# Narrower warm-up products, a moved instruction fetch and a new rule table in an attention and MLP kernel

## The chip, the core and the metric

The kernel runs on one core of a Trainium2 chip. Its engines are TensorE (PE in the profile, with its weight loads as PEld), VectorE (DVE), ScalarE (ACT), GpSimd (POOL) and SyncE (SP), which issues the DMA transfers; 16 DMA engines carry these. The time is device microseconds of one execution; the figure for a kernel is the median of several runs. The trace is of one profiled execution, whose span is a little longer than the runs without a profile.

## The reference, cut to what matters

```python
x = A_x                                        # [1, 2048, 640], bf16
xn = layernorm(x)
# attention: 32 heads of 20 columns
q, k, v = split(xn @ wqkv)                     # wqkv [640, 1920]
p = softmax(q @ k.T * 20 ** -0.5)              # 32 times 2048 x 2048
s = (p @ v).reshape(1, 2048, 640) @ wo
# token mixer: the MLP runs over the 2048 rows
h = layernorm(xn)
u = gelu(h.T @ w1 + b1)                        # w1 [2048, 1536]
y = (u @ w2 + b2).T                            # w2 [1536, 2048]
return x + s * silu(y)
```

The bulk is the exponential of 32 x 2048 x 2048 scores. ScalarE takes about three quarters of them, VectorE the rest, with an approximation that writes the bits of a bf16 number.

## The kernel before: the parts that matter here

The program is straight-line code. A scheduler written in Python decides at build time the order of each engine's instructions. It keeps a model of when each engine is free, and takes for each engine the ready candidate of the best priority.

```python
class Prog:
    def pe(self, fn, reads=(), writes=(), name="pe", cost=250.0, tail=None, w=None):
        t = self._add("pe", "pe", fn, reads, writes, name, cost=cost, tail=tail)
        self.pe_end = self.T["pe"]
        self.alog.append((t.t0, cost * 1.0 if w is None else w))
        return t

    def activity(self, T):          # modelled busy share of TensorE before T
        a = 0.0
        for t0, w in reversed(self.alog):
            if t0 < T - 3413.0:
                break
            a += w
        return a / 3413.0
```

Every 16 score tiles (WIN) one row of a table, PLAN, is read; each digit chooses the value of one option of the scheduler (slack, when a bank may be lent, and so on). The table was found by a search outside the kernel, on the model's time.

```python
    OPTS = (
        ("SLACK", (120.0, 40.0, 200.0, 320.0)),
        ("MINJ", (640.0, 320.0, 1000.0)),
        # ... (cut: 12 more)
    )
    PLAN = ("00200200000010", "02000000000000", ...)      # cut: 129 rows

    def tune(self, w):
        if w < len(self.PLAN):
            for (name, vals), i in zip(self.OPTS, self.PLAN[w]):
                setattr(self, name, vals[int(i)])
```

The model's cost of changing the way the PE array is divided, and of a DMA transpose (`nbytes` is None):

```python
        def pe_cost(mode, c):
            if pe_mode[0] != mode:
                pe_mode[0] = mode
                return c + max(0.0, (119.0 if mode == "st" else 100.0) - max(0.0, pr.T["pe"] - pr.pe_end))
            return c

        def dma(fn, reads, writes, name, nbytes, over=()):
            if nbytes is None:
                pr.dma(fn, reads=reads, writes=writes, name=name, cost=1320.0, over=over, tail=2700.0)
```

The start: x is loaded, normalized on VectorE block by block (16 blocks of 128 rows), and transposed into xnT: blocks 0 to 3 on TensorE, blocks 4 to 15 by one DMA transpose each, in batches of four. From xnT come the projections q, k and v of the first four heads; their scores are the first work for ScalarE's exponential.

```python
        def xTd_steps(b):
            dst = xnT_sb[:, :, b * 128:(b + 1) * 128]
            src = regC[:, b, :]
            return [("dma", lambda e: e.dma_start_transpose(dst, src), [S_(f"h{b}")], [S_(f"xTb{b}")], f"xTd{b}", None), ...]
```

Until then TensorE multiplies zeros to keep its clock up (`emit_warm`). Later on, where the model sees a gap and low activity, it adds products of zeros to the accumulator (`emit_fill`, four products at a time).

```python
        def emit_warm():
            pr.pe(lambda e: e.matmul(ps(AB), on_sb[:, 0:4, :], on_sb[:, :, :], start=True, stop=True),
                  reads=[S_("on")], writes=[bank_slot[AB]], name="warm", cost=pe_cost("full", 216.0) +
                  (214.0 if pr.T["pe"] < 4500.0 else 0.0), w=216.0)

        # in pe_cands, while the start lasts (ramp):
                    nxt = min([max(x[1], T) for x in c] + [1e18])
                    if not pv_seen and nxt - T > 260.0:
                        c.append((99.0, max(T, 1000.0), emit_warm))
                    elif pv_seen and nxt - T > (216.0 if pe_mode[0] == "pv" else 321.0) + self.FGAP and fill_ok() and (
                            pr.activity(T) < self.FACT):
                        c.append((99.0, T, emit_fill))
```

A last piece estimates how much work each engine has before it. The kernel stores it in `self.loads`, and nothing in the kernel calls it; the search does.

```python
        def loads():
            a, d = pr.T["act"], pr.T["dve"] + 601.0 * len(dop1)
            pe = pr.T["pe"] + 54.0 * len(avail)
            # ... (cut)
            return a - done_cost["act"], pe - done_cost["pe"], d - done_cost["dve"]
```

Of the kernel before, what the change touches and what calls it, by code (L numbers as in the profile page):

```python
# [39 lines left out]
class Prog:  # L40
# [7 lines left out]
    def __init__(self, nc, n_lanes=8):  # L48
        self.nc = nc
        self.n_lanes = n_lanes  # L50
        self.cengs = list(self.COMPUTE) + [f"d{i}" for i in range(n_lanes)]
        self.cidx_of = {c: i for i, c in enumerate(self.cengs)}
        self.tasks = {e: [] for e in self.COMPUTE}
        self.ctasks = {c: [] for c in self.cengs}
        self.gcount = 0
        self.lane_rr = 0
        self.known = {e: [0] * len(self.cengs) for e in self.COMPUTE}
        self.T = {e: 0.0 for e in self.COMPUTE}
        self.busy = {e: 0.0 for e in self.COMPUTE}
        self.pipe = 0.0  # L60
        self.pe_end = 0.0
        self.alog = []

    def lat(self, eng, src):
# [87 lines left out]
    def pe(self, fn, reads=(), writes=(), name="pe", cost=250.0, tail=None, w=None):  # L152
        t = self._add("pe", "pe", fn, reads, writes, name, cost=cost, tail=tail)
        self.pe_end = self.T["pe"]
        self.alog.append((t.t0, cost * 1.0 if w is None else w))
        return t

# [98 lines left out]
class _Kern:  # L256
# [9 lines left out]
    AB = 6  # L266
# [43 lines left out]
        ("GROT", (1, 0)),  # L310
    )
    PLAN = (
        "00200200000010", "02000000000000", "00000000000000", "00000000000010", "00000000000000", "00002200000000",
        "02002200000000", "01002200000000", "01024200101000", "00000000000000", "10000010000000", "12000010000000",
        "12203110110010", "00020010000010", "30000000000110", "30020020000110", "00020010000010", "10001400000000",
        "10001000000000", "12001010010000", "00000000000000", "02000000001000", "00000100010100", "00124100110110",
        "00124200111100", "00104300111000", "00020000000000", "00020010000000", "01020310000000", "01120310010000",
        "01010000100000", "00002200001000", "01002200001000", "10002000000000", "00000000000000", "00000300000000",
        "01004010000000", "12000210100000", "12104210100000", "00000200000000", "00121200000100", "00124200000100",
        "00124200000100", "00000400000000", "01100000000100", "00000000000000", "00000010101000", "01000010001000",  # L320
        "01000010010000", "01000010010000", "01000410010000", "02000000000110", "00020120000000", "00020220101000",
        "00220220101000", "10220210001000", "00002000000000", "00000000000000", "00102020001100", "00011200000100",
        "00000000000000", "02020200000000", "00000000000000", "10102000000010", "10100000000010", "10003000001000",
        "10003000000110", "10002300000110", "00020320000000", "20020000000000", "20220020000000", "20200020000010",
        "20200020000010", "20000320100010", "00010110100100", "01003410000000", "01003410110000", "00010000000000",
        "00002000000100", "02002000000100", "00020100000000", "00022300100000", "00000000000000", "00100000100000",
        "20100400100100", "00122010000000", "00004301010000", "00000400000010", "22001000000010", "00000000000000",
        "00000001000000", "00000200001100", "00010200000100", "10220210000000", "02100210000000", "00000020000000",
        "20013110000000", "20020310000000", "00000020110100", "00000000000000", "00003000001010", "00002100000000",
        "00002000010000", "10002020110010", "10203120100010", "02000400000000", "00110010010000", "02020000000000",  # L330
        "00110000101010", "10020000000100", "10110000010000", "00100000000000", "02120000000000", "00020020100000",
        "00020020100000", "00020100100010", "00000000000000", "00004100000010", "00000000000000", "21000400000000",
        "31020400000000", "00110201100000", "00000000100000", "02000000100010", "12000000110010", "02000020001000",
        "00000000000000", "01001000000000", "00000000000000",
    )
    PARTS = (2,)
    DX = (1, 2, 3)
# [74 lines left out]
    def schedule(self):  # L412
# [48 lines left out]
        def pe_cost(mode, c):  # L461
            if pe_mode[0] != mode:
                pe_mode[0] = mode
                return c + max(0.0, (119.0 if mode == "st" else 100.0) - max(0.0, pr.T["pe"] - pr.pe_end))
            return c

        def dma(fn, reads, writes, name, nbytes, over=()):
            if nbytes is None:
                pr.dma(fn, reads=reads, writes=writes, name=name, cost=1320.0, over=over, tail=2700.0)
            else:  # L470
                pr.dma(fn, reads=reads, writes=writes, name=name, cost=nbytes / 355.0, over=over)

# [580 lines left out]
        avail = []  # L1053
# [250 lines left out]
                      reads=[S_("zw"), S_("wp0"), S_("wp1")], writes=[bank_slot[AB]], name="pvz", cost=tot / 4, w=53.0)  # L1304
            stats["fill"] = stats.get("fill", 0) + 1

        def emit_warm():
            pr.pe(lambda e: e.matmul(ps(AB), on_sb[:, 0:4, :], on_sb[:, :, :], start=True, stop=True),
                  reads=[S_("on")], writes=[bank_slot[AB]], name="warm", cost=pe_cost("full", 216.0) +
                  (214.0 if pr.T["pe"] < 4500.0 else 0.0), w=216.0)  # L1310

        def emit_pv(items, quads):
            q = pv_pass[0]
# [595 lines left out]
            return c  # L1909

        def loads():
            a, d = pr.T["act"], pr.T["dve"] + 601.0 * len(dop1)
            pe = pr.T["pe"] + 54.0 * len(avail)
            for us, banks, grp in pexp:
                a += len(us) * 512 * 0.8335 + 50.0
                pe += 54.0 * len(us)
# [98 lines left out]
```

## Time and profile before

| | |
|---|---|
| median of 3 runs | 760.98 us (760.37 to 761.41) |
| span of the profiled execution | 762.1 us |
| granted TensorE clock, mean | 0.991 |
| products of warming (512 columns) | 27 |
| filler products | 48 |
| exponentials on ScalarE | 430 of 1024 columns, 232 of 1536 |
| score tiles on VectorE | 492 of 512 columns |

A line with busy times names the engine, its busy microseconds, and behind the x the number of instructions. The granted clock is TensorE's, as a share of full speed. In the DMA lines a queue has a number and a kind, then its packets, megabytes, and the time its packets took as a share of 16 engines; "hardware_dynamic" are the kernel's own transfers, "instruction" are packets of program code that the engines fetch while they run. A wait names the engine and line that waited, what it waited for, and us in total, times, and the longest. Line numbers are those of the kernel before; L1236 is ScalarE's exponential, L1207 the score products, L1308 the warm-up, L1302 the filler, L625 the projections q and k of the first four heads.

### The profile page before, as it was taken

The page shows a single profiled execution, that of the slowest core. Times are in us where ns is not written, and L with a number is a line of the kernel's source. Part 1 is how long each engine was busy: PE and PEld are TensorE (multiplying, and loading weights), DVE is VectorE, ACT ScalarE, POOL GpSimd, SP SyncE. Part 2 cuts the span into 40 slices and gives each one's busy share as a digit, 9 for nine tenths or more (in the row PEclk, how much of TensorE's full clock was granted, in tenths as well). Part 3 has the DMA queues.
Part 4 walks back from the last instruction along what each step waited for, and adds up shares of the span by engine and source line. Part 5 has one row for each costly group of instructions (what it writes and reads, how often), then busy time and mean ns, then how long its engine had stood idle before and what let it go on. Part 6 is the DMA issues. An engine that isn't in the chain of part 4 may idle for free.

```text
span 762.1 us, 22703 instructions
## 1 busy us (share of the span) xinstructions
PE 730.9 (96%) x10088; PEld 242.8 (32%) x10088; DVE 715.7 (94%) x1314; ACT 732.8 (96%) x684; POOL 15.9 (2%) x22
## 2 busy tenths in 40 slices
PE   8989999999999999999999999999999999999997
PEld 3332233323232323333223232333333333233322
DVE  8689999999999999999989999999999999999994
ACT  5889999999999999999999999999999999999994
POOL 4200000000000000000000000000000000000001
PEclk9899999999999999999999999999999999999999
DMA  9485110101120301211211112112133520041101
GB/s 240 62 127 132 37 35 13 43 6 36 38 62 13 74 14 38 64 31 19 69 37 20 30 44 64 43 45 66 40 80 70 116 82 13 9 144 46 47 14 69
DMA packets 117142, 42.52 MB, mean 56 GB/s; under 512 B 75300, under 2 KB 115876, under 8 KB 116996
## 3 DMA queue, kind: packets, MB, share of 16 engines
q1 hardware_dynamic: 117044, 41.07, 23.6%
q8 instruction: 79, 1.29, 0.8%
q14 instruction: 19, 0.16, 0.1%
HBM read 26.37 MB, written 10.22 MB: 48 GB/s over the span
## 4 chain that ended last, share of the span: by engine, by line
ACT 70%; PE 22%; DVE 6%; DMA 1%; issue 0%
ACT pt_sb L1236 69%; PE ps_all L1207 7%; PE ps_all L640 6%; PE ps_all L1287 6%; DVE dt_sb L1247 2%; PE ps_all L625 1%; DVE dt_sb L1271 1%; PE ps_all L925 1%; DMA xnT_sb<-regC 1%; ACT zt_sb L831 1%; ACT zt_sb L836 1%; DVE regC L940 1%; PE ps_all L733 0%; DVE regC L1606 0%; DVE bst_sb L527 0%; DMA regA<-in_A_x_dram 0%
## 5 line engine op out<-in xcount | busy, mean ns | idle before, releaser
L1236 ACT ACTIVATE pt_sb<-ps_all 128x1024 bf16<-128x1024 f32 (+1 forms) x662 | 713.8, 1219 | 8.8 <-PE ps_all L1207 7.3
L1247 DVE TENSOR_SCALAR dt_sb<-ps_all 128x512 uint16<-128x512 f32 x492 | 329.3, 683 | 19.8 <-PE ps_all L1207 18.4
L1207 PE MATMUL ps_all<-qk_sb 32*128 32x512 bf16 x2048 | 292.5, 386 | 18.0 <-ACT pt_sb L1236 13.8
L1271 DVE TENSOR_SCALAR dt_sb<-dt_sb 128x2048 uint16<-128x2048 uint16 x369 | 244.2, 685 | 1.4
L1207 PEld LDWEIGHTS ps_all<-qk_sb 32*128 32x128 bf16 x2048 | 75.8, 91 | 275.1 <-ACT pt_sb L1236 183.3
L1287 PE MATMUL ps_all<-pt_sb,v_sb 128*21 128x512 bf16 x1556 | 122.5, 383 | 0.7 <-DVE v_sb L1040 0.7
L1287 PE MATMUL ps_all<-dt_sb,vs_sb 128*21 128x512 bf16 x1476 | 123.0, 382 | 0.0
L640 PE MATMUL ps_all<-regC,regA 128*32 128x512 bf16 (+1 forms) x1536 | 69.4, 301 | 0.0
L640 PE MATMUL ps_all<-regB,regA 128*32 128x128 bf16 (+1 forms) x1536 | 68.2, 301 | 0.5 <-DVE dt_sb L1247 0.5
L640 PE MATMUL ps_all<-xnT_sb,wqk_sb 128*32 128x512 bf16 x640 | 50.1, 382 | 0.4 <-DVE zt_sb L810 0.3
L1287 PE MATMUL ps_all<-dt_sb,v_sb 128*21 128x512 bf16 x492 | 48.5, 384 | 0.7 <-DVE tr_sb L1399 0.6
L1287 PEld LDWEIGHTS ps_all<-pt_sb,v_sb 128*21 128x21 bf16 x1556 | 28.8, 90 | 49.3 <-issue 38.1
L1287 PEld LDWEIGHTS ps_all<-dt_sb,vs_sb 128*21 128x21 bf16 x1476 | 31.3, 91 | 40.3 <-issue 25.1
L640 PEld LDWEIGHTS ps_all<-regB,regA 128*32 128x32 bf16 x1536 | 28.5, 96 | 27.4 <-issue 12.3
L640 PEld LDWEIGHTS ps_all<-regC,regA 128*32 128x32 bf16 x1536 | 28.4, 96 | 26.5 <-issue 13.0
L925 PE MATMUL ps_all<-wv_sb,xnT_sb 128*128 128x128 bf16 (+3 forms) x160 | 29.7, 302 | 0.1
L1399 DVE STREAM_TRANSPOSE tr_sb<-ps_all 128x512 f32<-128x512 f32 x31 | 22.0, 710 | 0.2 <-PE ps_all L1287 0.2
L640 PE MATMUL ps_all<-wv_sb,xnT_sb 128*32 128x480 bf16 x320 | 22.0, 369 | 0.0
L640 PEld LDWEIGHTS ps_all<-xnT_sb,wqk_sb 128*32 128x32 bf16 x640 | 13.8, 95 | 19.9 <-issue 9.2
L1287 PEld LDWEIGHTS ps_all<-dt_sb,v_sb 128*21 128x21 bf16 x492 | 12.3, 90 | 24.0 <-issue 17.3
L1040 DVE CAST v_sb<-ps_all 128x480 bf16<-128x480 f32 (+1 forms) x24 | 14.3, 595 | 4.1 <-PE ps_all L733 4.1
L810 DVE TENSOR_SCALAR zt_sb<-ps_all,b2h_sb 128x512 bf16<-128x512 f32 (+1 forms) x32 | 17.0, 543 | 0.9 <-PE ps_all L640 0.8
(81 smaller groups left out, 287.8 us busy)
## 6 DMA issues: line engine op xcount, KB each, us to landing
regA<-in_B_w_dram SPq DMA_DIRECT2D x6, 1024.0 KB
regA<-in_B_w_dram SPq DMA_DIRECT2D x8, 768.0 KB
qk_sb<-qk_scratch_dram SPq DMA_DIRECT2D x56, 80.0 KB
qk_scratch_dram<-qs_sb SPq DMA_DIRECT2D x32, 128.0 KB
regA<-in_A_x_dram SPq DMA_DIRECT2D x6, 640.0 KB
ok_scratch_dram<-on_sb SPq DMA_DIRECT2D x96, 20.0 KB
out_dram<-regC SPq DMA_DIRECT2D x3, 640.0 KB
wqk_sb<-in_A_wqkv_dram SPq DMA_DIRECT2D x2, 480.0 KB
```

What stands on the lines that cost most here:

```text
L625: steps.append(("pe", lambda e, dc=dc, lhsT=lhsT: e.matmul(ps(bk, n), lhsT, xnT_sb[:, dc, tb * 512 + c0:tb * 512 + c0 + n], start=(dc == 0 ...
L640: fns.append(lambda e, c=c, e_=e_: e.matmul(oc(c, e_), lhsT[:, c:e_], rhs, start=start, stop=stop, tile_position=(0, c)))
L810: steps.append(("dve", lambda e, z=z, i=i, jj=jj: e.tensor_scalar(z[:, c0:c0 + n], ps(bk, n, i * n), 0.5, bias[:, jj:jj + 1], ALU.mult, AL ...
L831: steps.append(("act", lambda e: e.activation(tt_, tt_, AF.Tanh, scale=1.5957691216), [stt], [stt], f"th{j}", ac(n)))
L925: steps.append(("pe", lambda e, c=c, k=k: e.matmul(ap, oT_sb[0:k, c, b * 128:(b + 1) * 128], wo_ap[0:k, c, c0:c0 + n], start=(opens and c ...
L1040: return lambda e: e.tensor_copy(dst, src)
L1207: pr.pe(lambda e, outp=outp, lhsT=lhsT, rhs=rhs, g=g: e.matmul(outp, lhsT, rhs, start=True, stop=True, tile_position=(32 * g, 0)), reads=[ ...
L1236: tk = pr.act(lambda e: e.activation(outp, inp, AF.Exp, scale=math.log(2.0) / 128.0), reads=[bank_slot[b] for b in banks[:n]], writes=[S_( ...
L1247: tk = pr.dve(lambda e: e.tensor_scalar(w, src, WOFF, 0.0, ALU.add, ALU.max), reads=[bank_slot[bk]], writes=[S_(f"dt{d['tl'][0]}_{g}")], n ...
L1271: tk = pr.dve(lambda e: e.tensor_scalar(dst, src, dk, None, ALU.add), reads=[S_(f"dt{b0}_{g}") for g in range(4)], writes=[S_(f"dt{b}_{g}" ...
L1287: pr.pe(lambda e: e.matmul(outp, lhsT, rhs, start=(k == 0), stop=last, tile_position=(0, 32 * g)), reads=reads, writes=[bank_slot[AB]], na ...
L1399: steps.append(("dve", lambda e: e.transpose(tr_sb[:, :], ps(AB)), [bank_slot[AB]], [S_("tr")], f"epT{q}", 632.0))
```

## The change

The warm-up product becomes 192 columns wide instead of 512 and takes turns in three places of the bank; the scheduler's model then puts 69 of them where there were 27. As TensorE's program gets longer ahead of the first scores, the points at which it fetches its next block of instructions lie elsewhere in time. The constants of the model for changing the array's division and for the DMA transposes are set to other, measured, values. A count of moments of low activity after 45 us of modelled time goes into the search's estimate, and the table was searched anew (129 rows in both; only its first lines are shown).

```diff
+        self.low = 0
+        self.lowt = 0.0
...
     def pe(self, fn, reads=(), writes=(), name="pe", cost=250.0, tail=None, w=None):
         t = self._add("pe", "pe", fn, reads, writes, name, cost=cost, tail=tail)
         self.pe_end = self.T["pe"]
+        if t.t0 > 45000.0 and t.t0 - self.lowt > 3413.0 and self.activity(t.t0) < 0.36:
+            self.low += 1
+            self.lowt = t.t0
...
     PLAN = (
-        "00200200000010", "02000000000000", "00000000000000", "00000000000010", "00000000000000", "00002200000000",
-        "02002200000000", "01002200000000", "01024200101000", "00000000000000", "10000010000000", "12000010000000",
+        "00000000000010", "00000000000000", "00000000000010", "00000000000000", "00000410000000", "10010410000100",
+        "00004010011000", "20204010111000", "00000000000000", "02000020010010", "00000000000000", "00000010001000",
...   (all other rows, too)
-                return c + max(0.0, (119.0 if mode == "st" else 100.0) - max(0.0, pr.T["pe"] - pr.pe_end))
+                return c + max(0.0, (105.0 if mode == "st" else 113.0) - max(0.0, pr.T["pe"] - pr.pe_end))
...
-                pr.dma(fn, reads=reads, writes=writes, name=name, cost=1320.0, over=over, tail=2700.0)
+                pr.dma(fn, reads=reads, writes=writes, name=name, cost=1320.0, over=over, tail=3200.0)
...
+        nwarm = [0]
+
         def emit_warm():
-            pr.pe(lambda e: e.matmul(ps(AB), on_sb[:, 0:4, :], on_sb[:, :, :], start=True, stop=True),
-                  reads=[S_("on")], writes=[bank_slot[AB]], name="warm", cost=pe_cost("full", 216.0) +
-                  (214.0 if pr.T["pe"] < 4500.0 else 0.0), w=216.0)
+            off = 160 * (nwarm[0] % 3)
+            nwarm[0] += 1
+            pr.pe(lambda e: e.matmul(ps(AB, 192, off), on_sb[:, 0:4, :], on_sb[:, 0:6, :], start=True, stop=True),
+                  reads=[S_("on")], writes=[bank_slot[AB]], name="warm", cost=pe_cost("full", 81.0) +
+                  (80.0 if pr.T["pe"] < 4500.0 else 0.0), w=81.0)
...
         def loads():
-            a, d = pr.T["act"], pr.T["dve"] + 601.0 * len(dop1)
-            pe = pr.T["pe"] + 54.0 * len(avail)
+            lo = 1500.0 * pr.low
+            a, d = pr.T["act"] + lo, pr.T["dve"] + 601.0 * len(dop1) + lo
+            pe = pr.T["pe"] + 54.0 * len(avail) + lo
```

How the order of instructions changes: TensorE starts with 54 warm-up products (20 before), then ten transposes, 5 (2), ten transposes, 8 (3), 15 projections and one more before the first scores, as before. ScalarE has 434 exponentials of 1024 columns and 228 of 1536 and two more evictions; VectorE has 496 tiles of scores, 372 passes over four tiles (369 before) and two evictions fewer. Filler products are 100.

## The prediction

> **What bounds the kernel now.** I read the busy table first, then busy time by stage, then ScalarE's waits, then the DMA traffic of single microseconds.
>
> The page's first part, with busy time and share of the span:
>
> ```profile
> PE 730.9 (96%) x10088; PEld 242.8 (32%) x10088; DVE 715.7 (94%) x1314; ACT 732.8 (96%) x684; POOL 15.9 (2%) x22
> ```
>
> Three engines are within 2.4% of each other, so no engine can be relieved by much. What is left is idle time. The view by stage tells where (columns: stage, length, then busy time and instructions of PE, weight loads, DVE, ACT and POOL, granted clock, DMA share, GB/s):
>
> ```profile
> 0.00:13.54 13.54, 11.80 (x65) 5.19 (x66) 10.79 (x37) 4.30 (x6) 6.99 (x14) 1.00 0.88 277
> 13.54:20.55 7.01, 4.43 (x42) 2.17 (x42) 5.17 (x16) 5.54 (x5) 0.70 (x1) 1.00 1.00 146
> 20.55:28.88 8.33, 8.33 (x54) 3.13 (x53) 5.13 (x20) 6.29 (x6) 1.01 (x1) 0.59 0.24 48
> 28.88:40.21 11.33, 10.53 (x96) 4.82 (x94) 7.91 (x33) 10.62 (x10) 4.05 (x3) 1.00 0.50 73
> 40.21:47.50 7.29, 6.12 (x34) 2.15 (x35) 5.14 (x16) 4.22 (x5) 0.00 (x0) 0.77 0.73 167
> 47.50:742.00 694.50, 675.01 (x9689) 220.40 (x9686) 671.43 (x1178) 692.76 (x647) 0.88 (x1) 1.00 0.22 49
> 742.00:751.60 9.60, 9.60 (x96) 3.23 (x92) 3.10 (x5) 9.06 (x8) 0.00 (x0) 1.00 0.20 70
> 751.60:762.10 10.50, 5.05 (x26) 1.70 (x24) 6.99 (x16) 0.00 (x0) 2.26 (x2) 0.83 0.18 62
> ```
>
> Length minus ACT busy, stage by stage: 9.24, 1.47, 2.04, 0.71, 3.07, 1.74, 0.54, 10.50 us, 29.3 in all. In 694.5 us of steady state ScalarE stands still for 1.74: it sets the pace there, and the time is its work plus its idle at the two ends. Start (9.24) and tail (10.50) have the same structure in both kernels. The part that can move is the ramp from 13.54 to 47.50: 1.47 + 2.04 + 0.71 + 3.07 = 7.29 us.
>
> ScalarE's waits name score products as the ender of most of the ramp's idle:
>
> ```profile
> ACT pt_sb L1236 <- PE ps_all L1207: 7.3, 9, 1.7
> ACT qk_sb L1042 <- PE ps_all L625: 1.5, 1, 1.5
> ```
>
> Those scores need xnT, which comes in twelve DMA transposes, in batches of four (13.26 to 40.9 us). DMA by queue in five short windows: an undisturbed transpose in 27.1 to 28.2; one in 15.8 to 18.3; the middle of that, 16.7 to 18.1; one in 36.4 to 38.5; its middle, 37.2 to 38.3.
>
> ```profile
> q1 hardware_dynamic: 672, 0.16, 74.5%
> ...
> q1 hardware_dynamic: 672, 0.16, 109.1%
> q8 instruction: 1, 0.02, 3.6%
> ...
> DMA packets 29, 0.01 MB, mean 5 GB/s; under 512 B 29, under 2 KB 29, under 8 KB 29
> ...
> q1 hardware_dynamic: 672, 0.16, 111.9%
> q8 instruction: 1, 0.02, 3.1%
> ...
> DMA packets 31, 0.01 MB, mean 7 GB/s; under 512 B 31, under 2 KB 31, under 8 KB 31
> ```
>
> A transpose is 672 packets. Undisturbed ones start at 25.8, 27.1, 28.5 and 29.8: 1.35 us apart. The one met by an instruction packet at 15.8 lasts until 18.3, 2.5 us; the one met at 36.4 until 38.5, 2.1 us. In the middle of both nearly nothing moves, as if fifteen of the 16 DMA engines waited for the one that carries the instructions. So the first fetch costs batch 1 some 2.5 - 1.35 = 1.15 us, the second batch 3 some 2.1 - 1.35 = 0.75 us. Batch 1 and batch 3 are what the longest DMA pieces of the chain of waits are (4.99 us from 14.65, 2.64 us from 38.65).
>
> After both gaps in the products the granted clock falls: 0.59 in 20.55 to 28.88, 0.77 in 40.21 to 47.50.
>
> **What the Trainium skill says.** "Runtime: NRT & Kernel Launch", section "Instruction fetch mechanics": instructions come in blocks of 16 KiB, 256 instructions, on a DMA queue that the sequencer drives, and crossing a block is "mostly hidden". The trace agrees on the size (q8: 79 packets, 1.29 MB, 16.3 KB each; 2 x 10,088 product and weight-load records / 256 = 78.8); hidden it is not where a DMA transpose runs. "DMA: Bandwidth & Descriptors", section "Queues, rings and completion order": each DMA engine goes round its queues packet by packet, so a 16 KB packet stands ahead of the small ones on that engine; the trace's gap fits. "TensorE: Matmul & The Clock Gate", Part 1: half clock after a quiet window of about 3.4 us, full after a busy one. The trace agrees roughly: PE was busy 1.32 of the 3 us from 18 to 21, and from 21.5 to 27 the clock was near 0.50.
>
> **The change part by part.**
>
> *Warm-ups.* 27 products of 512 columns become 69 of 192: 42 more products, 84 more instructions with their weight loads, all but two groups of them before the first scores. The columns go from 13,824 to 13,248, so the warming work is equal: the first group ran 20 products in 5.99 us (0.43 us each cold, 0.21 warm); 54 of 192 columns are, scaled by columns, 21 x 0.16 + 33 x 0.08 = 6.0 us. It ends as before, near 7.2 to 7.4 us. Direct gain or cost: 0.
>
> *The fetch.* Before, it came when 89 products had started (15.85 us) and again after 89 + 131 = 220 (36.4 us). With the new order the 89th product is in the first projection after the warm-ups (10.62 us before). There the x and weight loads run, not a transpose; they end at 14.0 to 14.8 us, and one DMA engine's share may end up to an estimated 0.6 us later (half of the packet's 1.0 to 1.4 us, since it shares the engine), which delays batch 1 in part. I count 1.15 - 0.3 = 0.85 us won. The 220th product of the new order is in the projection of blocks 8 and 9, the one that started at 30.75 us before, as batch 2 ended (30.7). So the second fetch moves from batch 3 to the end of batch 2 or just after: of 0.75 us I count 0.6. Sum on the chain: 1.45 us.
>
> *Half clock.* With the wait in batch 1 shorter and eight filler products where four were, just at that wait, the first throttle probably goes, the second perhaps. ScalarE's idle then is 2.04 in the first slow stage; the last wait of the second, to 46.02, is 1.39. I count 1.5 us of 3.4: some of it is only moved to the wait for batch 3.
>
> *The table.* One more quad of score tiles goes to VectorE: exponentials of 1024 columns go from 430 to 434, of 1536 from 232 to 228. Busy per instruction with overlap: 431.8/430 = 1.004 and 347.0/232 = 1.496 us. ScalarE: 4 x 1.004 - 4 x 1.496 = -1.97 us, and two evictions move to it in the ramp, +0.59 + 0.38: net -1.0. VectorE: 4 x 0.669 + 3 x 0.662 = +4.7, less the evictions, to some 719 us, under ScalarE's. Filler products go from 48 to 100; 52/4 x 0.22 = 2.9 us of PE, in its gaps.
>
> *The rest.* The low-activity count and its use in the load estimate act on the search alone: nothing emitted reads them. The switching costs (105, 113) and the longer transpose tail (3200) change the order by what the scheduler believes.
>
> Sum: 1.45 + 1.5 + 1.0 = 3.95 us from 760.98: 757.0. The steady state has only 1.74 us of ScalarE idle to win and can lose more than that by a new table; I add 0.8.
>
> **The rivals.**
> 1. *The fetch only changes its victim.* It delays loads, and the second fetch hits batch 2 whole. For: the 220th product stands at the edge of batch 2; the loads run at 105% in 6 to 14 us. Against: loads do not freeze as transposes do, and batch 2 ends 4 us before batch 3 begins. The ramp gain shrinks to some 1 us, the time to 759 to 760.
> 2. *The new table is worse on the chip.* VectorE has 4.7 us more and was the chain's engine in 675 to 699; each VectorE eviction late holds a bank. For: VectorE is 94% busy; 44 of the 100 fillers stand late (products 9,625 to 9,763), so PE has gaps there. Against: ScalarE idled 1.74 us in 694.5 under the same kind of table. The time would be 761 to 763.
> 3. *The whole ramp wait goes.* Both throttles vanish and batch 3 comes early: the ramp's idle falls from 7.3 to 2, the time to 754.5.
>
> **Range and chances.** 757.8 us, 754.5 to 761.5 eight times in ten: the low end is rival 3, the high end rival 2 at its mildest, and the spread of before (760.37 to 761.41) is within it. 2% is 15.2 us, more than all the ramp's idle and the steady idle together, and slower by so much would need a new stall of 15 us: faster 0.01, within 0.98, slower 0.01.
>
> **What would show it.** The first instruction packet at 10 to 11 us with no gap in the transposes from 14.5; batch 1 done by 19.5 instead of 20.6; clock near 1.00 in 21 to 29; ScalarE's idle from its first exponential to 47.5 us between 3.5 and 5; ACT busy near 731.8. Wrong if a fetch again falls into a transpose of batch 1 or 3, if the half-clock stage stays, or if ScalarE's idle in steady state rises above 3 us.

## The result and the profile after

The changed kernel takes 757.34 us (median of 4 runs, 756.49 to 758.22) against 761.19 us for the kernel before in the same comparison (760.37 to 763.69): ratio 0.9944, 95% interval 0.9918 to 0.997. The profiled executions have spans of 756.4 and 762.1 us. The gain of 3.9 us is real and lies well within 2%.

The page's first part of the changed kernel, busy time and share of the span by engine:

```profile
PE 726.6 (96%) x10194; PEld 245.9 (33%) x10194; DVE 718.4 (95%) x1319; ACT 731.3 (97%) x686; POOL 15.7 (2%) x22
```

ScalarE has 1.5 us less work and VectorE 2.7 more, as a table that gives VectorE four more of the 2048 score tiles should make it. The view by stage of the changed kernel (columns as in the prediction: stage, length, busy time of PE, weight loads, DVE, ACT, POOL, granted clock, DMA share, GB/s):

```profile
0.00:13.54 13.54, 11.89 (x103) 9.46 (x103) 10.52 (x35) 3.75 (x5) 7.00 (x14) 1.00 0.86 277
13.54:20.55 7.01, 5.78 (x59) 2.72 (x61) 5.76 (x18) 6.94 (x7) 0.70 (x1) 1.00 0.97 146
20.55:28.88 8.33, 7.83 (x76) 3.58 (x68) 7.38 (x32) 7.94 (x9) 1.32 (x2) 1.00 0.61 77
28.88:40.21 11.33, 9.64 (x88) 4.38 (x86) 7.99 (x32) 9.75 (x11) 3.74 (x3) 1.00 0.67 145
40.21:47.50 7.29, 7.22 (x64) 2.69 (x62) 7.21 (x16) 7.29 (x8) 0.00 (x0) 1.00 0.64 77
47.50:742.00 694.50, 673.96 (x9742) 219.63 (x9741) 672.38 (x1177) 691.85 (x648) 0.63 (x1) 1.00 0.22 49
```

Length minus ACT busy: 9.79 in the start, 0.07 + 0.39 + 1.58 + 0.00 = 2.04 in the ramp, 2.65 in the steady state. Before it was 9.24, 7.29 and 1.74. So, between these two executions, the ramp gave 5.25 us, the start took 0.55 and the steady state 0.9 back; with 1.5 us less work and 0.4 less idle at the end that makes the 5.7 us between the two spans. The clock column has no 0.59 and no 0.77 any more. ScalarE's wait for scores, 7.3 us in nine times before, in the changed kernel:

```profile
ACT pt_sb L1241 <- PE ps_all L1212: 2.9, 4, 1.3
```

The fetch did not do what I had counted on. DMA by queue in three short windows of the changed kernel: 14.6 to 15.1 us, 16.5 to 17.5 us, and 28.2 to 30.8 us:

```profile
q8 instruction: 1, 0.02, 13.4%
...
DMA packets 69, 0.03 MB, mean 26 GB/s; under 512 B 61, under 2 KB 69, under 8 KB 69
...
q8 instruction: 1, 0.02, 3.7%
```

The first instruction packet starts at 14.95 us, at the very edge of batch 1. In the second window 61 packets of a transpose and 8 larger ones, of the loads of x, move in a whole microsecond: the last load packet ends at 17.1 us (before: 14.95), and the first transpose, under way since 15.1, ends at 17.6. Batch 1 is done at 20.6 us, exactly as before. The second fetch, at 28.36 us, falls into the last transpose of batch 2 and makes it last from 28.2 to 30.8.

What closed the wait instead is seen in the timeline of PE. The kernel before (start, length, engine, line, operation, count, and in brackets the idle time before it and what ended it):

```profile
16.88 0.39 PE L1207 MATMUL ps_all<-qk_sb 32*128 32x512 bf16 x2 [0.17 <-ACT pt_sb L1236]
19.68 0.50 PE L625 MATMUL ps_all<-xnT_sb,wp_sb 128*128 128x256 bf16 x3 [2.41 <-DMA xnT_sb<-regC]
20.11 0.39 PE L1207 MATMUL ps_all<-qk_sb 32*128 32x512 bf16 x3
```

And the changed kernel:

```profile
17.44 0.39 PE L1212 MATMUL ps_all<-qk_sb 32*128 32x512 bf16 x2 [0.20 <-ACT pt_sb L1241]
17.75 0.61 PE L1307 MATMUL ps_all<-wp_sb,zw_sb 128*21 128x512 bf16 x8
18.78 0.39 PE L1212 MATMUL ps_all<-qk_sb 32*128 32x512 bf16 x3 [0.41 <-ACT pt_sb L1241]
19.72 0.72 PE L630 MATMUL ps_all<-xnT_sb,wp_sb 128*128 128x256 bf16 x5 [0.55 <-DMA xnT_sb<-regC]
```

The data for the projection (L625, now L630) come at the same moment, 19.7 us. But before, the projection stood ahead of three scores that needed no transpose, and held them and ScalarE up. Now those scores and eight fillers stand ahead of it. VectorE's order differs likewise: before, the cast of the second part of this projection stood ahead of four normalizations, now two of them stand ahead of it (VectorE before):

```profile
23.90 0.42 DVE L1040 CAST qk_sb<-ps_all 128x256 bf16<-128x256 f32 x1 [1.89 <-PE ps_all L625]
24.24 1.51 DVE L545 TENSOR_SCALAR regC<-regA,st_sb 128x640 bf16<-128x640 bf16 x4
```

The place of the scores comes from the scheduler's constants (a transpose is believed to land 500 ns later; tail_only below has the same three scores ahead), which I had counted as nothing. The eight fillers come with the narrow warm-ups: warm_only has them, all_but_warm doesn't.

### The profile page after: what moved, and what is told of

Read it like the earlier page. It is cut to its first block, busy times and chain, and to the rows that moved or that the text cites. A ratio compares the mean times of both kernels' runs of the same rounds, so it can differ in the third digit from the quotient of the medians.

```text
span 756.4 us, 22917 instructions
## 1 busy us (share of the span) xinstructions
PE 726.6 (96%) x10194; PEld 245.9 (33%) x10194; DVE 718.4 (95%) x1319; ACT 731.3 (97%) x686; POOL 15.7 (2%) x22
## 4 chain that ended last, share of the span: by engine, by line
ACT 67%; PE 23%; SPq 4%; DVE 3%; DMA 3%; POOL 1%; issue 0%; DVEq 0%; ACTq 0%
ACT pt_sb L1241 65%; PE ps_all L1212 7%; PE ps_all L1292 7%; PE ps_all L645 7%; SPq L906 3%; DMA xnT_sb<-regC 1%; PE ps_all L930 1%; DMA regA<-in_B_w_dram 1%; ACT zt_sb L836 1%; DMA wqk_sb<-in_A_wqkv_dram 1%; DVE dt_sb L1252 1%; PE ps_all L630 1%; POOL st_sb L567 0%; SPq L1425 0%; DVE regC L1615 0%
## 5 line engine op out<-in xcount | busy, mean ns | idle before, releaser
L1252 DVE TENSOR_SCALAR dt_sb<-ps_all 128x512 uint16<-128x512 f32 x496 | 330.8, 681 | 17.1 <-PE ps_all L1212 15.6
L1212 PE MATMUL ps_all<-qk_sb 32*128 32x512 bf16 x2048 | 286.6, 384 | 18.7 <-ACT pt_sb L1241 14.5
L1212 PEld LDWEIGHTS ps_all<-qk_sb 32*128 32x128 bf16 x2048 | 73.9, 91 | 276.4 <-ACT pt_sb L1241 193.0
L645 PE MATMUL ps_all<-regC,regA 128*32 128x512 bf16 (+1 forms) x1536 | 65.9, 301 | 0.0
L645 PE MATMUL ps_all<-wv_sb,xnT_sb 128*32 128x480 bf16 x320 | 23.6, 369 | 0.2 <-DVE v_sb L1045 0.2
```

Source lines behind the costliest of these rows:

```text
L645: fns.append(lambda e, c=c, e_=e_: e.matmul(oc(c, e_), lhsT[:, c:e_], rhs, start=start, stop=stop, tile_position=(0, c)))
L1212: pr.pe(lambda e, outp=outp, lhsT=lhsT, rhs=rhs, g=g: e.matmul(outp, lhsT, rhs, start=True, stop=True, tile_position=(32 * g, 0)), reads=[ ...
L1252: tk = pr.dve(lambda e: e.tensor_scalar(w, src, WOFF, 0.0, ALU.add, ALU.max), reads=[bank_slot[bk]], writes=[S_(f"dt{d['tl'][0]}_{g}")], n ...
```

## The experiments

Theories: *fetch* (the place of the instruction fetches), *clock* (the half-clock stages after the waits), *order* (what stands ahead of the waits in the queues), *table* (ScalarE's share of the work). Ratios are to the kernel before in the same comparison, with the 95% interval.

### Which part of the change

**all_but_warm: the changed kernel with the wide warm-ups of before.**

```diff
-            pr.pe(lambda e: e.matmul(ps(AB, 192, off), on_sb[:, 0:4, :], on_sb[:, 0:6, :], ...   (69)
+            pr.pe(lambda e: e.matmul(ps(AB), on_sb[:, 0:4, :], on_sb[:, :, :], ...               (27)
```

> The changed kernel with the wide warm-ups of before. The same work on ScalarE and VectorE (434 and 228 exponentials), the fetches back at the places of before in the order (first near 16 to 17 us, second near 31), and the scheduler places no filler in the first wait. Fetch theory: batches 1 and 3 are hit, time 759.5 to 761. Clock theory: without the eight fillers the clock falls after the first wait, time 759 to 760.5. Table theory (the gain is in the order and the units): 757.3 to 758.

Measured: 757.27 us, 0.9952 (0.993 to 0.9973). The first fetch is back at 16.16 us, in batch 1, and the second, at 33.46, falls into batch 3; the eight fillers ahead of the wait for batch 1 are gone, too. ScalarE's and VectorE's orders are those of the changed kernel. The gain is all there without the narrow warm-ups and without the moved fetch. Three of its ten runs had a mean clock of 0.993 to 0.994 and took 3.7 us more than the others; none of the changed kernel's four did, which is too few to say that the warm-ups prevent it.

**warm_only: the kernel before with the narrow warm-ups alone** (the same edit the other way round).

> The kernel before with the narrow warm-ups alone, old table and constants. The order after the start is a new one, which the table was not searched for: 443 exponentials of 1024 and 227 of 1536 columns, by 1.004 and 1.496 us some 5.6 us more of ScalarE than before. Clock theory: clock near 1.00 in the ramp, as eight fillers stand in the first wait, ramp idle 2 to 4 us, time 761 to 763. Fetch theory: the same 761 to 763 with the fetches as in the changed kernel. If the table did not matter: 757 to 758.

Measured: 773.8 us, 1.015 (1.0122 to 1.0179). ScalarE has 443 exponentials of 1024 columns and 227 of 1536, and is busy 741.1 us. The warm-ups move every later decision of the scheduler, and a table found for one order gives a bad division of the work in another. By its time it says nothing on the fetch. But its ramp is short, with the constants of before, a projection ahead of the three scores as before, and a clock of 0.91 and 0.87 in two stages: 1.41 + 1.07 + 1.29 + 0.00 = 3.77 us of ScalarE idle.

```profile
13.54:20.55 7.01, 5.32 (x49) 2.26 (x50) 5.21 (x16) 5.60 (x6) 0.70 (x1) 0.91 0.82 153
20.55:28.88 8.33, 8.13 (x67) 3.33 (x66) 6.15 (x23) 7.26 (x8) 1.01 (x1) 0.87 0.24 49
```

**old_table: the changed kernel with the table of before.**

```diff
     PLAN = (
-        "00000000000010", "00000000000000", ...   (129 rows)
+        "00200200000010", "02000000000000", ...   (129 rows of before)
```

> The changed kernel with the table of before: warm-ups, switching costs and tail as in the change. The ramp should be that of the changed kernel (batch 2 from 24 us, clock near 1.00, ramp ScalarE idle near 2 us). ScalarE has 445 exponentials of 1024 columns and 223 of 1536, by the durations of the trace 1.6 us more than before and 3.6 us more than the changed kernel. Theory 'table' (ScalarE's work counts one for one and a table fits one order only): 760 to 762 us, 3 to 5 us over the changed kernel, so the ramp's gain is hidden by the table. Rival (the gain is all in the ramp, and some 2 us of ScalarE's work fits in its idle): within 1 us of the changed kernel.

Measured: 776.9 us, 1.0199 (1.0172 to 1.0226). Both expectations fell: it is 19.6 us over the changed kernel (15.3 over the kernel before), not 3 to 5. Busy time by engine:

```profile
PE 737.6 (95%) x10202; PEld 248.3 (32%) x10202; DVE 713.6 (92%) x1305; ACT 737.5 (95%) x693; POOL 15.7 (2%) x22
```

ScalarE has 6.2 us more than the changed kernel, and does its last exponential at 753.1 instead of 745.8 us. After it come 22.0 us of tail instead of 10.7: products, and VectorE's work on them, are left over. So 11.3 of the 18.6 us between the two spans are lost at the end of the program, where I had counted nothing. The ramp, however, is good: 0.13 + 1.37 + 0.74 + 0.00 = 2.24 us of ScalarE idle. So the short ramp doesn't need the new table, which mends the rest of the program for the new order.

**tail_only: the kernel before with the longer transpose tail alone.**

```diff
-                pr.dma(fn, ..., cost=1320.0, over=over, tail=2700.0)
+                pr.dma(fn, ..., cost=1320.0, over=over, tail=3200.0)
```

> The kernel before with the longer modelled tail of transposes (3200 in place of 2700) alone; table, switching costs and wide warm-ups as before. Read by stage, not by its time: theory 'the tail orders the ramp': three more score products stand ahead of the first projection, ScalarE's idle from 13.54 to 47.5 us falls from 7.3 to 2 to 3.5 us, although the fetch stays at 16 us. By its time it is over 770 us, since the table was searched for another order (as in the run with the narrow warm-ups alone and the run with the old table). Rival: the ramp's idle stays at 5 us or more, and the ramp's gain needs the table or the warm-ups.

Measured: 774.67 us, 1.0176 (1.0143 to 1.0209). Two of its stages:

```profile
13.54:20.55 7.01, 4.87 (x43) 2.44 (x43) 5.20 (x16) 6.88 (x6) 0.70 (x1) 0.94 1.10 143
20.55:28.88 8.33, 8.01 (x64) 2.51 (x63) 6.40 (x23) 6.48 (x7) 1.01 (x1) 0.84 0.33 66
```

The ramp's idle is 0.13 + 1.85 + 0.99 + 0.00 = 2.97 us with the fetch still at 16.3 us, as the theory *order* had it; what of the 7.29 us of before belongs to that one execution is said further down.

**switch_only: the kernel before with the two switching costs alone.**

```diff
-                return c + max(0.0, (119.0 if mode == "st" else 100.0) - ...
+                return c + max(0.0, (105.0 if mode == "st" else 113.0) - ...
```

> The kernel before with the two switching costs of the change alone (105 and 113). Read by stage: the ramp keeps before's order (a projection ahead of three scores), so ScalarE's idle from 13.54 to 47.5 us stays at 5 to 8 us and the granted clock falls below 0.9 in one stage at least. By its time 766 us or more for the table that no longer fits. Rival: the ramp's idle falls under 4 us with the switching costs too.

Measured: 786.86 us, 1.0336 (1.0302 to 1.037). My expectation for the ramp was wrong: idle there is 0.92 + 0.06 + 2.25 + 0.00 = 3.23 us, at full clock:

```profile
20.55:28.88 8.33, 8.23 (x80) 3.75 (x72) 7.31 (x28) 8.27 (x9) 1.01 (x1) 1.00 0.33 66
```

PE waited 1.92 us here for batch 1 (17.35 to 19.27), with the projection ahead of the three scores as before, and the clock stayed up. So it isn't only the tail that gives a short ramp, and a wait of such a length doesn't always cost the clock.

**tiny_fill: the changed kernel with the ramp's twelve fillers cut from 512 to 16 columns.**

```diff
-                outp = ps_all[32 * g:32 * g + DH + 1, AB * 512:AB * 512 + 512]
-                rhs = wp_sb[:, 0:2, :, :]
+                n_ = 16 if ramp[0] else 512
+                outp = ps_all[32 * g:32 * g + DH + 1, AB * 512:AB * 512 + n_]
+                rhs = wp_sb[:, 0, 0, 0:16] if ramp[0] else wp_sb[:, 0:2, :, :]
```

> The changed kernel with the fillers of the start (12 products) cut from 512 to 16 columns: order, number of instructions and fetches are the same, the work of the fillers is gone. Clock theory (the gain comes from keeping TensorE's clock up through the wait for the first DMA transposes): the clock falls to about half somewhere in 21 to 29 us, ScalarE's idle between its first exponential and 47.5 us rises from 2.0 to 4 us or more, time about 759 to 760. Order theory (the new order of instructions feeds batches 2 and 3 earlier by itself) and fetch theory: clock stays at 1.00 and the time stays at 757.3.

Measured: 757.03 us, 0.9943 (0.9922 to 0.9964). The clock in 20.55 to 28.88 us of its profile fell to 0.87, and one of its six runs, at a mean clock of 0.993, took 759.08 us; the median doesn't move. With that lost clock the ramp's idle is 0.02 + 0.92 + 0.94 + 0.00 = 1.88 us. The fillers are not what the gain hangs on.

### Fetch, clock and order, each alone on the kernel before

Each of the first four leaves the table, VectorE's share and ScalarE's work as before: no other decision of the scheduler moves. hoist_split joins two of them; split_after is an edit of the changed kernel.

**split_before: 19 warm-ups, each split in six products of 85 columns** (95 more products, on 32 weight columns instead of 128; 510 columns streamed for 512).

```diff
+            if 1 < nwarm[0] <= 20:
+                for h in range(6):
+                    pr.pe(lambda e, h=h: e.matmul(ps_all[0:32, AB * 512 + 85 * h:AB * 512 + 85 * h + 85], on_sb[:, 0, :], ...   85 columns
+                return
```

> The kernel before with 19 of its warm-up products each split in six of 85 columns: 95 more products before the ramp, the same warming work; nothing else moves. Theory 'fetch': the first fetch moves to 10 us or earlier, the second to about 23 us between batches 1 and 2, the third to about 42 us after batch 3; batch 1 ends at about 19.5 us instead of 20.6 and batch 3 at about 40 instead of 40.9, the second of these partly carried on from the first; the time falls by 1 to 2 us, to about 759.8, more if the shorter wait also spares the half clock. Rivals 'order' and 'clock' alone: the transposes get shorter, but the statistics and casts of the next batch hold the chain, and the time falls by less than 0.5 us.

Measured: 758.34 us, 0.9952 (0.9938 to 0.9967). The fetches start at 10.21, 22.94 and 41.16 us, none of them within a batch; batches 2 and 3 are over at 29.5 and 36.9 us instead of 30.8 and 40.8. Two stages, and PE's wait for batch 1:

```profile
13.54:20.55 7.01, 5.61 (x55) 2.60 (x57) 5.95 (x18) 6.61 (x8) 0.70 (x1) 1.00 0.93 163
20.55:28.88 8.33, 8.12 (x80) 3.58 (x68) 7.20 (x28) 8.33 (x9) 1.01 (x1) 1.00 0.34 69
```

```profile
19.13 0.50 PE L625 MATMUL ps_all<-xnT_sb,wp_sb 128*128 128x256 bf16 x3 [1.24 <-DMA xnT_sb<-regC]
```

The wait is 1.24 instead of 2.41 us (half of that because the data come at 19.1 instead of 19.7 us, the other half because the scores ahead of it ran 0.6 us later), the clock stays at 1.00, and the ramp's idle is 0.40 + 0.00 + 1.36 + 0.00 = 1.76 us. Moving the fetch alone is worth about what the whole change is worth, if it really leaves the batches.

**before_fill: 28 more fillers ahead of two K projections of the ramp.**

```diff
+                if j.name in ("k0_1a", "k0_3") and j.i == 1 and fill_ok():
+                    for z in range(4):
+                        for g in range(4):
+                            pr.pe(... e.matmul(outp, zw_sb[:, 0:DH + 1], rhs, start=False, stop=False, ...), name="pvx", cost=0.0, w=0.0)
```

> The kernel before with 28 more filler products of zeros, ahead of the first and the third K projections of the ramp, in gaps where PE waits; nothing else moves. Theory 'clock' (the half-clock stages after the two waits for transposes cost 2 to 2.5 us of the 4 us): the granted clock of 20.55 to 28.88 us rises from 0.59 to over 0.85, the mean clock to 0.998 or more in nearly every run, and the time falls by 2 to 2.5 us, to about 758.9. Theory 'fetch': the transposes of batch 1 still end at 20.6 us, the clock only fills a wait that stands anyway, and the time falls by less than 0.5 us. Theory 'order': batch 2 begins at 25.9 us as before where the products of the cast still wait, or comes 1 us earlier because they run at full clock; then up to 1 us of gain comes from there.

Measured: 759.28 us, 0.9974 (0.9962 to 0.9986): 2.0 us, as the theory *clock* had it, from products of zeros alone. Two stages of the profiled execution:

```profile
20.55:28.88 8.33, 8.33 (x52) 3.25 (x52) 4.42 (x18) 5.72 (x5) 1.01 (x1) 0.59 0.27 54
40.21:47.50 7.29, 7.25 (x67) 2.96 (x63) 7.06 (x23) 5.34 (x7) 0.00 (x0) 1.00 0.93 189
```

The second stage keeps the clock (0.77 before); the first didn't in this execution, against my expectation: a wait of 1.75 us is left. But of its 22 runs, 14 had a mean clock of 0.998 or more, against 11 of 83 of the kernel before.

**swap_norm: two normalizations of VectorE ahead of the cast that waits for PE.**

```diff
+            if s[0] == "ev" and j.name == "k0_1":
+                ...   the first two normalizations of blocks 8 to 11 are put into VectorE's queue here, ahead of the cast
```

> The kernel before with one exchange on VectorE: two of the four normalisations of blocks 8 to 11 stand ahead of the cast of the second part of k0_1, as in the changed kernel; products and ScalarE's work keep their order. Theory 'order' (the cast, which waits for PE, holds up the normalisations and so the transposes of batch 2): batch 2 begins near 24.2 us instead of 25.9, the statistics of blocks 12 to 15 begin near 25 us instead of 27.2, the ramp's ScalarE idle falls by 1 to 2 us, the time by 1 to 1.5 us, to about 759.8. Rival 'fetch': the time follows where the instruction fetches fall, which is the same here as before (15.9 and 36.5 us): batch 1 is as long as before, and the time stays within 0.5 us of the kernel before. Rival 'clock': the half-clock stage stays, so the time stays within 0.5 us too.

Measured: 760.96 us, 0.9995 (0.9979 to 1.0011): nothing. VectorE's timeline:

```profile
23.86 0.80 DVE L545 TENSOR_SCALAR regC<-regA,st_sb 128x640 bf16<-128x640 bf16 x2 [0.95 <-POOL st_sb L541]
25.31 0.42 DVE L1040 CAST qk_sb<-ps_all 128x256 bf16<-128x256 f32 x1 [0.65 <-PE ps_all L625]
25.65 0.80 DVE L545 TENSOR_SCALAR regC<-regA,st_sb 128x640 bf16<-128x640 bf16 x2
```

The two run earlier in the queue, but the statistics before them had come late too, and the cast with the other two behind it still waits for PE at half clock. VectorE's order in this place is not the cause alone.

**hoist: three scores ahead of the five products of the projection.** That is the only difference in all queues.

```diff
+            if j.name == "k0_1a" and j.i == 0:
+                for g in range(3):      # the scores of chunk 2, planned after the third product of the projection
+                    early.append(pr.pe(... matmul(ps(g), lhsT, rhs, ...), name=f"st0_2_{g}", cost=0.0))
```

> The kernel before with one exchange in the order of the products: the three score products that stood among the five of the first K projection of the ramp (line 625) stand ahead of them, as in the changed kernel; ScalarE's and VectorE's orders and all else stay. Theory 'order on PE' (in before a projection that waits for the transposes of batch 1 stands in PE's queue ahead of scores that could run): ScalarE's idle in 13.54 to 20.55 us falls from 1.47 to under 0.3, PE's wait of 2.41 us at 17.3 shrinks below 2.0 with scores ahead of it, and the time falls by 1.2 to 3 us, to 758.5 to 760, the more the oftener the half clock is spared. Rival 'fetch': the fetch stays at 16 us, batch 1 ends at 20.6 us, and the chain goes on from there: the scores run earlier, but the same time is lost at the next wait, and the time stays within 0.5 us of the kernel before.

Measured: 760.01 us, 0.9989 (0.9977 to 1.0002): inconclusive, at most 1.8 us (0.23%). PE's timeline, and below it ScalarE's next wait:

```profile
18.14 0.39 PE L1882 MATMUL ps_all<-qk_sb 32*128 32x512 bf16 x3 [0.95 <-ACT pt_sb L1246]
19.46 1.25 PE L625 MATMUL ps_all<-xnT_sb,wp_sb 128*128 128x256 bf16 x5 [0.92 <-DMA xnT_sb<-regC]
```

```profile
22.62 6.88 ACT L1246 ACTIVATE pt_sb<-ps_all 128x1024 bf16<-128x1024 f32 x6 [2.28 <-PE ps_all L1217]
```

The wait of 2.41 us is now two of 0.95 and 0.92, and ScalarE's 1.47 us of idle in 13.54 to 20.55 are 0.21. But ScalarE then waits 2.28 us for the next scores: the idle time came back one wait later, at a clock of 0.89 in 20.55 to 28.88 us. At equal clock (the table below) 0.5 to 1.0 us are left of the gain, and 2.4 at 0.995, of two runs. Neither theory had the whole of it.

**hoist_split: hoist and split_before together.**

> The kernel before with that exchange and with the 19 warm-ups split in six, so that no fetch falls into batches 1 and 3. If the order on PE and the fetch remove the same wait, the gains do not add: about 757.5 to 758.3 us, no more than 1 us under the kernel with the split alone (758.3). If they are separate costs they add: 3.2 plus 1.2 to 2, about 756.5.

Measured: 757.52 us, 0.9955 (0.9941 to 0.9968), beside 0.9952 for the split alone. No added gain is seen. But hoist alone gave so little that the sum (0.9952 x 0.9989 = 0.9941) is the very end of this interval: that they don't add isn't shown.

**split_after: the changed kernel, 45 of its warm-ups split in two**, which puts the first fetch at 11.43 and the second at 22.33 us, between batches 1 and 2.

```diff
+            if 2 < nwarm[0] <= 47:
+                for h in (0, 1):
+                    pr.pe(... matmul(ps_all[0:32, AB * 512 + off + 96 * h:...], on_sb[:, 0, :], on_sb[:, 3 * h:3 * h + 3, :], ...), cost=c / 2)
+                return
```

> The changed kernel with 45 warm-ups split into two of 96 columns on 32 weight columns: same columns streamed, 45 products more ahead of everything. Request theory for the fetch (asked for when some 90 to 100 products have started, then waiting on its DMA engine behind the packets of large loads): first fetch between 6 and 11 us, second near 22.5 us between batches 1 and 2, third near 36.5 us after batch 3. Fetch theory of the gain: batch 1 ends by 19.4 instead of 20.6 us, the last transpose of batch 2 lasts 1.0 instead of 2.7 us, time 756.0 to 756.5. Clock theory: the wait that is left is small (2.0 us), time 756.5 to 757.3.

Measured: 756.5 us, 0.9931 (0.9909 to 0.9953), the lowest median of all. The last transpose of batch 2 lasts 0.9 us, as the theory had it, but batch 1 ends at 20.1 us, not by 19.4. Its interval overlaps that of the changed kernel (0.9918 to 0.997), so it is at best slightly ahead.

### Time against clock

Each run has a mean granted clock, and the time of a kernel follows it. Median span in us (number of runs) of single runs, in six of the columns:

| mean clock | 0.989 | 0.995 | 0.997 | 0.998 | 0.999 | 1.000 |
|---|---|---|---|---|---|---|
| before | 763.1 (6) | 760.2 (12) | 759.1 (21) | 758.1 (7) | 757.5 (4) | none |
| swap_norm | 763.1 (1) | | 759.0 (8) | 758.1 (1) | | |
| before_fill | | 760.2 (4) | 758.5 (3) | 757.2 (4) | 757.4 (6) | 757.1 (4) |
| hoist | | 757.8 (2) | 758.1 (6) | | 757.0 (2) | |
| split_before | | 757.6 (1) | | 756.5 (7) | 756.5 (4) | 756.8 (1) |
| hoist_split | | 758.7 (1) | | 755.6 (7) | 756.1 (2) | 755.9 (1) |
| all_but_warm | | | | | 755.4 (1) | 755.4 (6) |
| the change | | | | | 755.3 (1) | 755.8 (3) |
| tiny_fill | | | 755.5 (1) | 756.0 (1) | 754.8 (2) | 755.0 (1) |
| split_after | | | | 754.4 (1) | 754.2 (2) | 755.2 (2) |

For the kernel before, 0.001 of mean clock goes with (763.1 - 757.5) / 10 = 0.56 us. The middle one of its 83 runs is at 0.996, and none reaches 1.000; those of the change lie at 0.999 to 1.000. That is 3.5 steps, 2.0 us. A longer wait can lower the clock, too, so this is what goes with the clock and not its effect alone. At equal clock (0.999, for the change all four runs) the change is some 757.5 - 755.6 = 1.9 us ahead. The filler products gain mostly by the clock: at equal clock they are within 1 us of before, and equal at 0.999. The split gains by both, 1.0 to 1.6 us at equal clock (0.998 and 0.999).

The profiles show both parts. Those of hoist, before_fill, before and swap_norm (the order of before, with one edit each or none) have 3.41, 6.83, 10.24 and 13.65 us of half clock in the ramp and 4.33, 5.73, 7.29 and 8.50 us of ScalarE idle there: an estimated 1.4 us for each 3.41. With 3.41 us of half clock tail_only has 2.97, old_table 2.24 and tiny_fill 1.88 us of idle. So an order can make the ramp short even where the clock is lost.

The spread itself fits the Trainium skill, "TensorE: Matmul & The Clock Gate", Part 1, section "What's actually happening": the window that decides on the clock runs freely and isn't tied to the program, so the same wait can fall differently into it from run to run. The traces agree on its length: half clock comes in stretches of 3.41 us (hoist, from 18.99 us), 6.83 (before, from 21.32) and 10.24 (swap_norm, from 19.46), one, two and three times the 3413 ns of that section. That it is the window's place which makes the spread (0.989 to 0.999 for one kernel), no run here shows.

## Why the prediction was right or wrong

The time was right: 757.8 predicted, 757.34 measured; a gain of 3.95 in the sum, 3.2 with the allowance of 0.8, against 3.9. That is in part luck: one term, the fetch, failed, and a gain from the order, which had no term of its own, made up for it.

*Warm-ups at zero: right.* all_but_warm has the same time as the change. The 0.55 us of the start isn't theirs: with the same narrow warm-ups the start's idle is 9.29 us in old_table and 9.79 in the change.

*The fetch, 1.45 us: the step that failed.* I had it that the fetch follows the count of products, and that in the loads "one DMA engine's share may end up to an estimated 0.6 us later". The first half holds: product 91, then every 128th after it, calls the packet; between 80 and 200 us the packets of both kernels start within 0.6 us of the start of these products. In the changed kernel product 91 starts at 11.4 us, close to the 10 to 11 us that I expected. But the packet itself started at 14.95 and overlaps the first transpose of batch 1, under way since 15.1, so that one of my signs of being wrong came true at the edge: while loads fill the DMA engines (share 1.06 and about 365 GB/s from 8 to 14 us) the packet comes 3 to 4 us later than its product. So it is in other kernels that reach product 91 in the loads: from 6.5 to 10.2 us in split_before, from 8.0 to 11.4 in split_after, from 7.4 to 10.6 in hoist_split. In before product 91 starts at 16.0, after the loads, and the packet comes at once. The cited section "Queues, rings and completion order" of "DMA: Bandwidth & Descriptors" offers a cause: a DMA engine drains a whole packet of one queue before it turns to the next; that this is the cause of the 3 to 4 us was not tried. The loads ended 17.1 - 14.95 = 2.2 us later than before, where I had counted 0.3. That the packet delayed them isn't shown: in tiny_fill, with the packet at 14.48, they end at 15.2, and in before_fill, with the packet after them, at 16.55. And the second fetch went to the end of batch 2, as I said, but cost it 30.8 - 28.2 - 0.9 = 1.7 us (an undisturbed transpose takes 0.9) instead of nothing much. In place of the 1.45 us the step gave nothing that can be seen: batch 1 ends at 20.6 us as before, and all_but_warm, whose fetches fall into batches 1 and 3 (16.16 and 33.46 us), is as fast.

That a fetch within a batch costs time was right, though, in the order of before: where the fetches do leave the batches (split_before), 3.2 us go, close to the 1.45 + 1.5 I had for fetch and clock together. The change didn't do that: its first packet is at the edge of batch 1, its second within batch 2. And in its order less hangs on them: split_after, with both out of the batches, is 0.8 us ahead by the medians, which is within the intervals.

*The half clock, 1.5 us: right in its sign and nearly in its size*, 2.0 us by the table above. I had named a shorter wait in batch 1 and the eight fillers. PE's wait did shrink, from 2.41 us to 0.41 and 0.55, but by what stands ahead of it: the data came at 19.7 us in both. The fillers alone don't explain it, as all_but_warm keeps its clock in seven of ten runs without these eight. The last stage too kept its clock, "the second perhaps".

*The table, 1.0 us, and 0.8 for the steady state: right.* ScalarE's work fell by 1.5 us, and the steady idle rose from 1.74 to 2.65 us, 0.9. Where I read four more score tiles as the table's effect, old_table shows that this is the small part: a table for another order costs 19.6 us.

*The switching costs and the tail, zero: too little, by an amount that stays open.* I had said that they "change the order by what the scheduler believes" and gave that no number. tail_only and switch_only, each with wide warm-ups and the first fetch in batch 1, have 2.97 and 3.23 us of ramp idle instead of 7.29. But these are single executions; an estimated 4.4 of the 7.29 us are typical (see *The signs*), and warm_only, with the constants of before, has 3.77. So each part of the change alone has a shorter ramp in its one profile. What is shown is that the constants and the table together, without the narrow warm-ups and the moved fetch, have the whole gain (all_but_warm); what each is worth in the ramp is not. Which exchange in the queues does it stays open: neither the three scores nor the two normalizations (at most 1.8 and 1.6 us by their intervals) is enough alone, and the two together were not tried.

*The signs.* ACT busy 731.8 predicted, 731.3 measured; clock near 1.00 in 21 to 29 us, so it was; steady idle under 3, 2.65. The ramp's idle, 3.5 to 5, was 2.04, the value of rival 3, and yet the time isn't rival 3's 754.5. The profiled execution of before, at a clock of 0.991, was itself 762.1 - 759.2 = 2.9 us above the median of its runs (760.98 us is a span of 759.2, the difference being 1.7 to 1.9 in nearly every run). So probably some 2.9 of the 7.29 us of ramp idle that I took as the stock were of this one execution: hoist, at a clock of 0.997, has 4.33 us.

Rival 1, the fetch changing only its victim, describes what happened to the second fetch; that the first delays the loads isn't shown, and its 759 to 760 us took the fetch as the whole of the ramp. Rival 2 didn't come: the new table holds the steady state to within 0.9 us.

What stays open: how often the change loses the clock (no run in 4; 3 in 10 with wide warm-ups), and why PE's waits of 1.75 and 1.92 us cost the clock in one kernel's profile and not in the other's.

## What to carry to other kernels

An engine with an in-order queue turns a belief of the scheduler into a wait: if a transfer lands later than modelled, the first instruction that needs it blocks those behind it that don't. The Trainium skill says of products that they stay in program order ("TensorE: Matmul & The Clock Gate", Part 2, "Step-by-step: what each phase is for"), and the 2.41 us show it: the three scores behind them could have run 1.5 us earlier, as they did at 18.1 us in hoist; when a diff changes a scheduler's constants, compare the orders of the queues before giving that part a zero. And before a profile's idle time is taken as the stock to win from, see where its span lies among the runs: here probably 2.9 of 7.3 us belonged to one execution. A moved instruction fetch has to be followed to where its packet lands, not to where the program asks for it.

## What the runs showed of the hardware that was not expected

- An instruction packet of 16.3 KB is 3 to 4 us late when its turn comes within full loads: product 91 started at 11.4 us, the packet at 14.95. Between 80 and 200 us, at a DMA share of 0.12, it comes within 0.6 us.
- A transpose that began before the last load packet was through stopped until it was: in before_fill, with the instruction packet only at 17.0, from 15.9 to 16.55 us, in the changed kernel from 16.3 to 17.1. When the loads end differs between kernels and executions, 14.95 to 17.1 us, for a reason that stays open.
- A mean clock lower by 0.001 over the whole kernel goes with 0.56 us of time, over ten steps in 83 runs of the kernel before: so small a difference in that column shows in the time.
- A wait of 1.92 us left the clock at 1.00 in one profile, one of 1.75 us was followed by 0.59 in another.
